# Separate semaphores for the output transposes of the last but one group in a cross-network kernel

## The chip, the cores and the metric

One NeuronCore of a Trainium2 chip. The metric is the device time of one execution in microseconds (us); lower is better. Before the change, three runs gave a median of 479.59 us (479.14 to 480.7). All were classed as fast; a one-core program whose run is within 1.5% of its fastest is classed so.

## The reference

A deep-and-cross network: 16384 rows of 416 features (bf16), six layers, each a full product with a 416 x 416 matrix, followed by a product and a sum element by element.

```python
B, F, D, L = 16384, 26, 16, 6          # Din = 26 * 16 = 416
def reference(x0, ws, bs):
    x = x0
    for l in range(ws.shape[0]):
        proj = jnp.einsum('bd,de->be', x, ws[l]) + bs[l]
        x = x0 * proj + x
    return x
```

## The kernel before

The rows are cut in 8 groups of 2048. A group is held transposed: features on the partitions (three tiles `t` of 128 features and a rest of 32), rows along the free dimension. TensorE multiplies, ScalarE adds the bias on the way out of PSUM, VectorE multiplies by `x0` and adds `x`. The pairs (group, layer) are interleaved, so that TensorE always has one to work on.

At the end of a group its result must be turned back, rows on the partitions. For groups 0 to 6 the DMA engines do this, with one transposing DMA for each feature tile into the staging tile `ost`, and one for the rest into `ot3`. Then `ost` is stored to HBM. Group 6 is "the last but one"; its store is cut in two column parts. Group 7, the last, is computed row-wise in its last layer, needs no turning, and is stored in five pieces.

```python
def output(g):
    s, s3 = xset[(g, L)], xtail[(g, L)]
    def turn(t):
        add("sp", lambda h: h.dma_start_transpose(
            ost[:, :, t * P:(t + 1) * P], xs[s][:, t * GC:(t + 1) * GC]),
            reads=[("x", s, t, j) for j in range(NJ)], writes=[("ost", t)], lane="ot", batch=g)

    turn(0)
    add("sp", lambda h: h.dma_start_transpose(ot3[:, :, :], x3s[s3][:, :]),
        reads=[("x3", s3)], writes=["ot3"], lane="ot3", batch=g)
    if g < LAST - 1:
        spread("pool")                        # ot3 -> the last 32 columns of ost
    turn(1)
    turn(2)
    if g < LAST - 1:
        store(g, 0, D, range(NT + 1))
    else:
        store(g, 0, 2 * P, (0, 1))            # first column part: 0..255, 1024 KB
    ...
# after the last tile of group 7, layer 4:
    spread("act")
    store(LAST - 1, 2 * P, D, (NT - 1, NT))   # second column part: 256..415, 640 KB
    ...                                       # last layer of group 7, row-wise:
    nat_store(0, 0, NJ)                       # three stores of 416 KB from SP, as they get done
    ...
        if j == 2:
            nat_store(kk, 0, 3)               # 312 KB from SP
    nat_store(kk, 3, 4, "act")                # 104 KB from ScalarE
```

A DMA's completion is counted on a semaphore per *lane*. The kernel assumes nothing about the order in which DMAs of the same lane and batch finish, so a count cannot tell them apart, and whoever needs one of them waits for the full count of the batch:

```python
for k, (key, ops) in enumerate(batches):
    n += 16 * len(ops)
    for op in ops:
        total[id(op)] = (n, ops)              # a wait for any op waits for all of its batch
```

SP (SyncE, which here only issues DMAs) works through its instructions in the order of the program: in the trace below it issues nothing from 461.19 to 464.71 us, while the first store of group 6 waits.

## Time and profile before

| quantity | before |
|---|---|
| median of 3 runs | 479.59 us |
| span of the profiled execution | 478.5 us |
| TensorE busy | 97% of the span |
| end of VectorE's last addition | 472.91 us |
| from there to the end of the span, called **the tail** below | 5.55 us |

The profile's page of the kernel before, the busy times by engine and the chain of waits that ended last:

```profile
PE 462.7 (97%) x3317; PEld 196.0 (41%) x3371; DVE 403.7 (84%) x696; ACT 342.3 (72%) x372; POOL 7.1 (1%) x15
...
PE 93%; DVE 2%; ACT 2%; issue 1%; POOL 0%; POOLq 0%
```

TensorE bounds the kernel as a whole. But the change is in the last microseconds, and there another limit holds. The timeline of the end, kernel before (start in us, length in us, engine, line, operation; SPq and ACTq are issues of DMAs, whose length is the time that the issuing engine spends on it, not the transfer):

```profile
456.79 4.40 SPq L637 DMA_TRANSPOSE ost<-x  x2
464.71 1.92 SPq L670 DMA_DIRECT2D out_dram<-ost  x2
466.67 6.85 SPq L866 DMA_DIRECT2D out_dram<-x  x4
...
472.53 0.38 DVE L859 TENSOR_TENSOR x<-x,x 128x416 bf16<-128x416 bf16 x1
472.94 0.37 ACTq L866 DMA_DIRECT2D out_dram<-x  x1
```

SP issues transposes 1 and 2 from 456.79 on (done with it at 461.19), then nothing until 464.71, then the two column parts of group 6 and four pieces of group 7. The waits of SP's DMA queue from 456 us on (who waited for what: us in total, times, longest):

```profile
SPq L670 <- DMA ost<-x: 3.5, 1, 3.5
```

The 3.5 us are the wait of the first column part for a transpose. By the completion records of the trace, transpose 1 landed at 461.22 us and transpose 2 at 464.70. The first part needs transposes 0 and 1 only.

The busy time by stretches of the end, kernel before (of use here are the last two columns: the mean busy share of the 16 DMA engines and GB/s; a packet that stands still counts as busy and packets overlap, so the share can pass 1, and the engines are taken as full here only where it is 1 or more and the GB/s are high too):

```profile
core 0: us, PE busy (x) PEld busy (x) DVE busy (x) ACT busy (x) POOL busy (x), PEclk, DMA share, GB/s
462.00:463.00 1.00, 1.00 (x17) 0.43 (x14) 0.78 (x2) 1.00 (x3) 0.00 (x0) 1.00 0.21 5
463.00:464.00 1.00, 1.00 (x13) 0.51 (x6) 0.97 (x3) 1.00 (x3) 0.00 (x0) 1.00 0.85 189
464.00:465.00 1.00, 1.00 (x7) 0.58 (x6) 0.90 (x2) 1.00 (x3) 0.00 (x0) 1.00 0.24 51
465.00:466.00 1.00, 1.00 (x13) 0.24 (x11) 0.83 (x3) 1.00 (x3) 0.00 (x0) 1.00 0.31 93
466.00:469.00 3.00, 3.00 (x23) 1.40 (x22) 2.93 (x6) 2.15 (x5) 0.00 (x0) 1.00 1.06 306
469.00:472.00 3.00, 1.76 (x11) 0.78 (x8) 2.57 (x6) 2.07 (x4) 0.00 (x0) 1.00 1.25 251
472.00:477.00 5.00, 0.00 (x0) 0.00 (x0) 0.87 (x3) 0.00 (x0) 0.00 (x0) 0.80 1.10 326
477.00:478.50 1.50, 0.00 (x0) 0.00 (x0) 0.00 (x0) 0.00 (x0) 0.00 (x0) 0.50 0.04 12
```

From 466 to 477 us the DMA engines are full without a break, and the last 4 us of that have no arithmetic at all. The end of the span is the end of that flow. Ahead of it are two poorer stretches: 462-463 (5 GB/s, a hole in the middle of transpose 2) and 464-466 (51 and 93 GB/s, between the end of transpose 2 and the first packets of the first store).

### The profile page before, as it was taken

The page shows a single profiled execution, that of the slowest core. Times are in us where ns is not written, and L with a number is a line of the kernel's source. Part 1 is how long each engine was busy: PE and PEld are TensorE (multiplying, and loading weights), DVE is VectorE, ACT ScalarE, POOL GpSimd, SP SyncE. Part 2 cuts the span into 40 slices and gives each one's busy share as a digit, 9 for nine tenths or more (in the row PEclk, how much of TensorE's full clock was granted, in tenths as well). Part 3 has the DMA queues.
Part 4 walks back from the last instruction along what each step waited for, and adds up shares of the span by engine and source line. Part 5 has one row for each costly group of instructions (what it writes and reads, how often), then busy time and mean ns, then how long its engine had stood idle before and what let it go on. Part 6 is the DMA issues. An engine that isn't in the chain of part 4 may idle for free.

```text
span 478.5 us, 8341 instructions
## 1 busy us (share of the span) xinstructions
PE 462.7 (97%) x3317; PEld 196.0 (41%) x3371; DVE 403.7 (84%) x696; ACT 342.3 (72%) x372; POOL 7.1 (1%) x15
## 2 busy tenths in 40 slices
PE   8999999999999999999999999999999999999993
PEld 6344444444443444444444444444444444434441
DVE  2888888888888888898889869888888888888894
ACT  4677777777777777777777777777777777767783
POOL 1000000000000000000000000000000000000000
PEclk9999999999999999999999999999999999999998
DMA  8986930730102477389219922870000237027889
GB/s 234 173 174 143 186 78 1 138 84 1 34 1 46 77 211 153 77 181 232 53 40 216 202 71 39 193 232 0 2 25 11 41 63 216 0 45 190 180 149 264
DMA packets 140379, 53.31 MB, mean 111 GB/s; under 512 B 114346, under 2 KB 139444, under 8 KB 140340
## 3 DMA queue, kind: packets, MB, share of 16 engines
q1 hardware_dynamic: 139592, 52.24, 49.0%
q10 hardware_dynamic: 748, 0.54, 0.4%
q8 instruction: 26, 0.43, 0.3%
q14 instruction: 13, 0.11, 0.1%
HBM read 5.97 MB, written 13.63 MB: 41 GB/s over the span
## 4 chain that ended last, share of the span: by engine, by line
PE 93%; DVE 2%; ACT 2%; issue 1%; POOL 0%; POOLq 0%
PE ps L456 75%; PE ps L477 7%; PE ps L497 6%; ACT tw L394 2%; PE ps L793 1%; PE ps L471 1%; DVE x L408 1%; PE ps L561 1%; DVE tw L403 1%; PE ps L541 1%; PE ps L488 1%; DVE x L859 0%; DVE x L853 0%; ACT x L565 0%; PE ps L804 0%
## 5 line engine op out<-in xcount | busy, mean ns | idle before, releaser
L394 ACT ACTIVATE tw<-ps,bias 128x1024 bf16<-128x1024 f32 (+1 forms) x295 | 299.8, 1071 | 119.8 <-PE ps L477 75.7
L456 PE MATMUL ps<-x,wm 128*128 128x512 bf16 x1638 | 372.2, 380 | 5.6 <-issue 3.7
L456 PEld LDWEIGHTS ps<-x,wm 128*128 128x128 bf16 x1692 | 159.1, 98 | 213.6 <-issue 28.8
L403 DVE TENSOR_TENSOR tw<-tw,x 128x1024 bf16<-128x1024 bf16 (+1 forms) x285 | 193.0, 686 | 53.4 <-ACT tw L394 53.1
L408 DVE TENSOR_TENSOR x<-tw,x 128x1024 bf16<-128x1024 bf16 (+1 forms) x285 | 181.9, 679 | 0.0
L477 PE MATMUL ps<-x,w 32*128 32x512 bf16 x512 | 39.2, 379 | 0.0
L497 PE MATMUL ps<-x,wm 128*32 128x512 bf16 x564 | 33.0, 380 | 0.0
L434 ACT ACTIVATE ts<-ps,bias 128x512 bf16<-128x512 f32 x47 | 28.8, 701 | 0.0
L438 DVE TENSOR_TENSOR x<-ts,x 128x512 bf16<-128x512 bf16 x47 | 18.8, 422 | 3.6 <-DMA x<-x 3.6
L497 PEld LDWEIGHTS ps<-x,wm 128*32 128x32 bf16 x564 | 13.8, 96 | 17.6 <-issue 5.3
L477 PEld LDWEIGHTS ps<-x,w 32*128 32x128 bf16 x512 | 7.8, 92 | 27.6 <-issue 27.1
L436 DVE TENSOR_TENSOR ts<-ts,x 128x512 bf16<-128x512 bf16 x47 | 18.7, 421 | 0.0
L663 POOL COPY ost<-ot 128x512 bf16<-128x512 bf16 x6 | 5.7, 943 | 422.6 <-DMA ot<-x 422.6
L793 PE MATMUL ps<-wm,x 128*128 128x416 bf16 x48 | 9.4, 340 | 0.0
L847 ACT ACTIVATE x<-ps 128x416 bf16<-128x416 f32 x16 | 7.7, 531 | 2.0 <-PE ps L793 1.9
L568 DVE COPY x<-ps 128x512 bf16<-128x512 bf16 x4 | 1.7, 425 | 8.8 <-PE ps L561 8.8
L565 ACT ACTIVATE x<-ps 128x512 bf16<-128x512 bf16 x8 | 4.2, 598 | 5.7 <-PE ps L561 5.7
L793 PEld LDWEIGHTS ps<-wm,x 128*128 128x128 bf16 x48 | 4.4, 98 | 4.1 <-issue 1.0
L488 PE MATMUL ps<-x,w 32*32 32x512 bf16 x188 | 5.9, 374 | 0.0
L471 PE MATMUL ps<-x,w 32*32 32x512 bf16 x208 | 5.6, 385 | 0.0
L561 PE MATMUL ps<-ident,x 128*128 128x128 bf16 x64 | 5.3, 243 | 0.3 <-ACT x L565 0.3
L853 DVE TENSOR_TENSOR x<-x,x 128x832 bf16<-128x832 bf16 (+1 forms) x9 | 4.9, 540 | 0.7 <-ACT x L847 0.6
(38 smaller groups left out, 35.9 us busy)
## 6 DMA issues: line engine op xcount, KB each, us to landing
out_dram<-ost SPq DMA_DIRECT2D x6, 1664.0 KB, 7.0
x<-in_x_dram SPq DMA_DIRECT2D x7, 416.0 KB, 8.0
x<-x SPq DMA_DIRECT2D x24, 96.0 KB, 2.2
wm<-in_ws_dram SPq DMA_DIRECT2D x5, 312.0 KB, 3.3
x<-x SPq DMA_DIRECT2D x22, 64.0 KB, 2.0
out_dram<-x SPq DMA_DIRECT2D x3, 416.0 KB, 5.6
out_dram<-ost SPq DMA_DIRECT2D x1, 1024.0 KB, 5.2
x<-ost SPq DMA_DIRECT2D x28, 32.0 KB, 2.3
```

Source lines behind the costliest of these rows:

```text
L394: add("act", lambda h, a=a, w=w, b0=b0: h.activation(tw[r][:, a * CH:(a + w) * CH], psum[:, b0 * CH:(b0 + w) * CH], ACT_F.Identity, bias=b ...
L403: add("dve", lambda h, a=a, e=e: h.tensor_tensor(tw[r][:, a * CH:e * CH], tw[r][:, a * CH:e * CH], x0s[s0][:, i * GC + a * CH:i * GC + e * ...
L408: add("dve", lambda h, a=a, e=e: h.tensor_tensor(xs[so][:, i * GC + a * CH:i * GC + e * CH], tw[r][:, a * CH:e * CH], src(i, a, e), ALU.ad ...
L434: add("act", lambda h: h.activation(ts[r][:, :], bank(b), ACT_F.Identity, bias=bias[:, 3, l:l + 1], scale=1.0), reads=[("ps", b), "bias"], ...
L436: add("dve", lambda h: h.tensor_tensor(ts[r][:, :], ts[r][:, :], x03, ALU.mult), reads=[("ts", r)] + tok0, writes=[("ts", r)], release=True)
L438: add("dve", lambda h: h.tensor_tensor(x3s[so][:, :], ts[r][:, :], res, ALU.add), reads=[("ts", r)] + rtok, writes=[("x3", so), ("x3", so, ...
L456: add("pe", lambda h, t=t, j=j: h.matmul(bank(banks[j]), wm[l][:, t, ecols], src(t, j, j + 1), start=(first and t == 0), stop=(not first a ...
L471: add("pe", lambda h, q=q, j=j, r=r, c=c, o=o: h.matmul(psum[o, banks[j] * CH:(banks[j] + 1) * CH], w3[l][q, i * P + c * T32:i * P + (c + ...
L477: add("pe", lambda h, q=q, j=j, r=r: h.matmul(bank(banks[j]), w3[l][q, ecols], src[q, :], start=first, stop=not first, tile_position=(r * ...
L488: add("pe", lambda h, l=l, b=b, s3=s3, ri=ri, qi=qi, ro=ro, qo=qo: h.matmul(psum[qo, b * CH:(b + 1) * CH], w3[l][qi, NT * P:D], s3[qi, :], ...
L497: add("pe", lambda h, t=t, j=j, src=src, l=l, b=b, ro=ro, qo=qo: h.matmul(psum[qo, b * CH:(b + 1) * CH], wm[l][:, t, NT * P:D], src(t, j, ...
L793: add("pe", lambda h, t=t: h.matmul(bank(b, n=D), xcol(t, j, kk), wm[l][:, t, :], start=(first and t == 0), stop=(not first and t == NT - 1)),
```

## The change

Intent: give each output transpose of group 6 its own semaphore, so that the first column part can wait for transposes 0 and 1 only, and go out earlier.

```diff
         def turn(t):
             add("sp", lambda h: h.dma_start_transpose(
                 ost[:, :, t * P:(t + 1) * P], xs[s][:, t * GC:(t + 1) * GC]),
-                reads=[("x", s, t, j) for j in range(NJ)], writes=[("ost", t)], lane="ot", batch=g)
+                reads=[("x", s, t, j) for j in range(NJ)], writes=[("ost", t)],
+                lane="ot" if g < LAST - 1 else f"ot_{t}", batch=g)
```

The order of instructions is the same on every engine; only waits differ. Below the change, line numbers are one higher (L670 becomes L671).

## The prediction

> **What bounds the kernel now.** Most of the span is TensorE: the page gives PE 97% busy, and the chain of waits is 93% PE. The change touches nothing there. It acts on the last 17 us. In the timeline the last matmul ends about 470.7 us and the last VectorE addition at 472.9, but the span ends at 478.5; the rest is output DMA. The windows view shows a DMA share of 1.06, 1.25 and 1.10 in 466-469, 469-472 and 472-477 us, at 306, 251 and 326 GB/s: from 466 to 477 all 16 DMA engines are full. So the tail is bound by the volume of the last seven stores (1024, 640, three of 416, 312 and 104 KB, 3.4 MB) and by when it starts to flow.
>
> **What starts it late.** The last but one group's three output transposes share one semaphore, and a wait is for its full count. In the trace's DMA records the second transpose (columns 128-255) lands at 461.2 us, the third at 464.7. The first store (columns 0-255, 1024 KB) needs only the first two, but is issued at 464.71, when the third lands; its first packets move at about 465.55. SP waits 3.5 us there (waits of the DMA queue).
>
> **What the change does.** No instruction is added, removed or moved; only waits differ. The first store waits for transposes 0 and 1; the second (columns 256-415) newly waits for transpose 2 beside ScalarE's spread copy, done at 460.1. SP pays for one or two more waits, at most 0.1 us. The first store can be issued when SP has issued the third transpose (461.19) and the second has landed: about 461.3, 3.4 us earlier. The second goes at about 464.75 instead of 465.15.
>
> **How much of 3.4 us survives.** The first store's packets stand behind the third transpose's in the same queue. The Trainium skill, "DMA: Bandwidth & Descriptors", section "Queues, rings and completion order", says that descriptors of one ring are taken in order; this trace agrees as far as it shows (a weight load issued behind a transpose began to move at 19.3 us, when the transpose's packets ran out). The third transpose's packets run until 464.4 us, with a hole at 461.9-463.1 (5 GB/s in the window 462-463) beside an instruction fetch. I expect the store not to fill it: in a like hole near 13 us ScalarE's queued copies stood still too. So the full stretch starts at 464.4 or slightly earlier instead of 465.55, and the same 3.4 MB follow at the same rates. Estimated gain: 1.15 us; up to 1 us more if the store does fill the hole. Above about 1.9 us nothing is left to win: the last stores are issued at 472.3 and 472.9, when their data is ready, and latency and their own transfer follow.
>
> **Prediction.** 478.4 us (gain 1.2 of 479.6, 0.25%), 8 in 10 between 477.4 and 479.5. Faster by over 2%: 0.01; within 2%: 0.985; slower by over 2%: 0.005.
>
> **What would show it.** First store issued near 461.3; second near 464.75, or up to 1 us later if the third transpose is delayed; DMA engines full from about 464.4; last landing about 476.7 instead of 477.9; PE, ACT and DVE unchanged up to 472.9.
>
> **What would make it wrong.** The third transpose slowed so much by the store's packets that the second store, and SP's queue behind it, is late and opens a hole; the store filling the hole (gain near 2 us); an instruction fetch at another moment; noise (479.1 to 480.7) larger than the gain.

## The result, and the profile after

| | before | after |
|---|---|---|
| median of 6 runs | 479.81 us | 478.80 us |
| lowest to highest | 479.14 to 480.70 | 478.15 to 479.41 |
| ratio of fast runs (95% interval) | | 0.998 (0.9966 to 0.9994) |
| span of the profiled execution | 478.5 | 477.6 |
| end of VectorE's last addition | 472.91 | 473.59 |
| tail | 5.55 us | 4.02 us |

A ratio is the mean time of one kernel's fast runs over the mean of the other's of the same rounds, so it is not quite the ratio of the medians. The change gains about 1 us, 0.2%.

The span falls by 0.85 us only, though the tail falls by 1.53. The rest, 0.68 us, is the start of this execution: TensorE waited 1.40 us for the first weights and began its first products at 7.66 us, against 6.60 us with no wait ahead of them in before. That is the lottery of the start (the runs of the experiments show how large it is), so from here on times are also given **relative to the end of VectorE's last addition**, which takes the start out.

The page after, the same two lines:

```profile
PE 462.0 (97%) x3317; PEld 195.7 (41%) x3371; DVE 404.1 (85%) x696; ACT 342.3 (72%) x372; POOL 6.5 (1%) x15
...
PE 92%; ACT 2%; DVE 2%; DMA 1%; issue 1%; ACTq 0%
```

The timeline of the end, after:

```profile
457.47 4.45 SPq L637 DMA_TRANSPOSE ost<-x  x2
462.02 0.97 SPq L671 DMA_DIRECT2D out_dram<-ost  x1
465.35 0.52 SPq L671 DMA_DIRECT2D out_dram<-ost  x1
465.92 7.37 SPq L867 DMA_DIRECT2D out_dram<-x  x4
...
473.21 0.38 DVE L860 TENSOR_TENSOR x<-x,x 128x416 bf16<-128x416 bf16 x1
473.62 0.37 ACTq L867 DMA_DIRECT2D out_dram<-x  x1
```

The first column part is now issued at 462.02 (less 0.68 for the start: 461.34 on the clock of before, against 464.71). The second part goes at 465.35, or 464.67 against 465.15. The waits of SP's DMA queue, after, the line that answers to the 3.5 us:

```profile
SPq L167 <- DMA ost<-x: 2.3, 1, 2.3
```

SP waits as before for transpose 2, but now only ahead of the second part (L167 is the helper's line for a separate wait instruction). The stretches of the end, after:

```profile
core 0: us, PE busy (x) PEld busy (x) DVE busy (x) ACT busy (x) POOL busy (x), PEclk, DMA share, GB/s
462.00:463.00 1.00, 1.00 (x16) 0.83 (x14) 1.00 (x3) 0.53 (x2) 0.00 (x0) 1.00 2.60 132
463.00:464.00 1.00, 1.00 (x14) 0.24 (x11) 0.78 (x2) 1.00 (x3) 0.00 (x0) 1.00 0.12 19
464.00:465.00 1.00, 1.00 (x7) 0.58 (x6) 0.97 (x3) 1.00 (x3) 0.00 (x0) 1.00 1.25 301
465.00:466.00 1.00, 1.00 (x7) 0.39 (x4) 0.76 (x3) 1.00 (x4) 0.00 (x0) 1.00 1.15 347
466.00:469.00 3.00, 3.00 (x29) 1.33 (x28) 2.90 (x6) 2.52 (x6) 0.00 (x0) 1.00 1.22 279
469.00:472.00 3.00, 2.45 (x20) 1.09 (x12) 2.60 (x5) 2.39 (x5) 0.00 (x0) 1.00 1.22 265
472.00:476.00 4.00, 0.00 (x0) 0.00 (x0) 1.52 (x5) 0.00 (x0) 0.00 (x0) 1.00 1.12 332
476.00:477.60 1.60, 0.00 (x0) 0.00 (x0) 0.00 (x0) 0.00 (x0) 0.00 (x0) 0.58 0.05 14
```

The poor stretch between the transpose and the stores is gone: 301 and 347 GB/s from 464 to 466. The hole in transpose 2 is still there (463-464, 19 GB/s) and is not filled, although the first store had been issued at 462.02. (The share of 2.60 in 462-463, at only 132 GB/s, is no full flow: packets of the transpose stood still there for up to 1.5 us each by their records.)

The trace records every DMA packet with its start, queue and size. Worked out from these records, for this kernel and all that follow (us relative to the end of VectorE's last addition; "98%" is when 98% of the store packets have started; "fetch" is the start of the 16 KB instruction fetches in the last 24 us):

```
run            tail  transpose 2  transposes'  first store  98% of  last    fetch
                     landed       last packet  packet       them    packet
before         5.55  -8.21        -8.70        -7.25        3.82    4.39    -11.40
after          4.02  -8.31        -8.79        -8.83        2.17    2.91    -11.36
e0_after       3.95  -8.38        -8.87        -8.91        2.10    2.84    -11.47
e10_after      4.21  -8.08        -8.58        -8.62        2.39    3.11    -11.15
e1_wait_all    5.46  -8.34        -8.83        -7.33        3.74    4.30    -11.41
e2_one_store   4.40  -8.15        -8.63        -7.13        2.77    3.22    -11.45
e3_no_first    2.52  -8.21        -8.70        -7.20        1.29    1.56    -11.36
e4_act_queue   3.96  -8.35        -8.84        -8.88        2.12    2.86    -11.43
e5_rows        3.62  -8.90,-8.08  -8.61        -7.89        2.01    2.53    -11.63
e6_fetch       3.79  -9.26        -9.75        -9.93        1.29    2.67    -20.07, -3.76
e7_rows_fetch  3.59  -10.37,-9.18 -9.64        -9.37        1.34    2.49    -20.02, -2.55
e8_fewer       4.49  -7.25        -9.27        -9.87        1.66    3.39    -9.26
e9_rows_fewer  3.26  -10.41,-7.80 -8.38        -8.43        1.55    2.17    -10.56
```

(Where the third transpose was cut in two halves, both landings are given.) The first two lines hold the explanation. Before, the stores' first packet came 1.45 us after the transposes' last one: 0.49 us until the completion was seen (-8.70 to -8.21), the rest from there through the issue to the first packet (-7.25). After, it comes as the transpose runs out, with no gap (16 of the store's packets start before the transpose's last one). The flow of the 3.41 MB of stores takes the same time in both: 11.64 us before (-7.25 to 4.39) and 11.74 us after (-8.83 to 2.91). So the tail is shorter by the shift of the flow's start, 1.58 us, less the 0.10, and with 0.05 us less from the last packet to the end of the span: 1.53.

Each tail is read from one profiled execution. How well it repeats can be seen from the kernels with the same flow: 5.55 and 5.46 in before and e1_wait_all, 3.95 to 4.21 in the three traces of the changed kernel and in e4_act_queue.

### The profile page after: what moved, and what is told of

Its sections match the earlier page's. It is cut to its first block, busy times and chain, and to the rows that moved or that the text cites. A ratio compares the mean times of both kernels' runs of the same rounds, so it can differ in the third digit from the quotient of the medians.

```text
span 477.6 us, 8343 instructions
## 1 busy us (share of the span) xinstructions
PE 462.0 (97%) x3317; PEld 195.7 (41%) x3371; DVE 404.1 (85%) x696; ACT 342.3 (72%) x372; POOL 6.5 (1%) x15
## 4 chain that ended last, share of the span: by engine, by line
PE 92%; ACT 2%; DVE 2%; DMA 1%; issue 1%; ACTq 0%
PE ps L456 75%; PE ps L477 7%; PE ps L497 6%; ACT tw L394 2%; DMA wm<-in_ws_dram 1%; PE ps L794 1%; PE ps L471 1%; DVE x L408 1%; DVE tw L403 1%; PE ps L488 1%; PE ps L561 0%; DVE x L860 0%; DVE x L854 0%; ACT x L565 0%; PE ps L805 0%
```

## The experiments

Two explanations stood against each other. **Theory A**: the end is the end of a DMA flow of fixed volume at the rate of its packets; the change gains the idle time before the flow. **Rivals**: B, the semaphores matter by themselves; C, SP's in-order queue sets the end, and the change gains because SP gets to the last group's stores earlier. Later came the hole in the third transpose: D, the instruction fetch that lies in it causes it; E, it is the transpose's own. Eleven runs were made, in three calls on chips 5, 7 and 5; each call shares its runs of the kernel before (medians 480.35, 480.44 and 480.14 us). All their executions were fast (e4_act_queue has four, e9_rows_fewer five, the others six).

### e0_after and e10_after: the changed kernel again

No edit.

> The changed kernel again, for an interval beside the other runs of this chip. Theory A (the tail is bound by the volume of the stores; the change gains the 1.15 us in which the DMA engines stood empty before the first store, and a little rate): about 1.2 to 1.5 us below before, ratio 0.997. The tail, from the end of VectorE's last addition to the end of the span, was 5.5 us before and 4.0 after; it should be 4.0 again, whatever the start of the run does.

> The changed kernel once more, as the neighbour of these two on the same chip: tail 4.0, ratio 0.997.

Measured: medians 479.01 and 479.68 us, ratios 0.997 (0.9945 to 0.9995) and 0.998 (0.9951 to 1.0008), tails 3.95 and 4.21. The gain repeats in the tail. In time the medians lie 1.34 and 0.46 us below those of before, and the second interval holds 1.0. What also shows is how noisy the start is. VectorE's last addition ended at 472.33 us in the first and at 474.95 us in the second, 2.6 us apart in the same kernel. TensorE's first products in the timeline of e0_after (start, length):

```profile
6.38 1.46 PE L456 MATMUL ps<-x,wm 128*128 128x512 bf16 x6
```

The same six products in the timeline of e10_after, with the idle time ahead of them and what ended it:

```profile
7.56 2.72 PE L456 MATMUL ps<-x,wm 128*128 128x512 bf16 x6 [0.79 <-DMA wm<-in_ws_dram]
```

In the second they start 1.2 us later, after a wait for the first weights, and the same six matmuls then take nearly twice as long. The runs of e10_after spread from 477.54 to 481.8 us. A difference of 1 us in the tail is clear in one trace, and hardly so in six times.

### e1_wait_all: the semaphores without the earlier issue

```diff
-            store(g, 0, 2 * P, (0, 1))
+            store(g, 0, 2 * P, (0, 1, 2))
```

> The change's three semaphores, but the first store waits for all three. Theory A (the earlier issue of the first store is the whole gain): as before, ratio 1.000, tail 5.5 us, first store issued when the third transpose lands, packets about 0.85 us later. Rival B (the separate semaphores or the other wait counts matter by themselves, for example by ending a wait sooner on SP or by a moved start of the run): as the change, ratio 0.997, tail 4.0.

Measured: 479.86 us, ratio 0.9983 (0.9964 to 1.0001), tail 5.46, first store packet at -7.33. The tail and the packets are those of before, with three semaphores in place. So B falls, by the trace: the earlier issue is the change's gain in the tail. The times would not settle it: the ratio of 0.9983 is about the change's own 0.998, its interval holds 1.0, and the median lies 0.49 us below that of before although the tail is that of before, which shows what the noise can do.

### e2_one_store: the same start, larger packets

In the kernel before, the two column parts are made one store:

```diff
-            store(g, 0, 2 * P, (0, 1))
+            pass
...
-    store(LAST - 1, 2 * P, D, (NT - 1, NT))
+    store(LAST - 1, 0, D, range(NT + 1))
```

> The kernel before, with the two stores of the last but one group made one of 1664 KB (packets of 832 bytes in place of 512 and 320), issued when the third transpose has landed. Theory A (volume at the rate of its packet size): in before the 1024 KB took about 3.4 us and the 640 KB 2.7 us of full DMA engines; 1664 KB at the 331 GB/s of the 832 byte packets take 5.15 us, so 0.9 us less: ratio 0.998, tail about 4.6 us, with the start of the flow as late as before. Rival C (what counts is when SP can issue the last group's stores, and the change gained because SP's queue is freed earlier): SP issues the last group's stores about 0.4 us earlier than in before, so at most 0.4 us.

Measured: 479.35 us, ratio 0.9974 (0.995 to 0.9997), tail 4.40, so 1.15 us shorter than before, where 0.9 was expected. The flow starts as late as in before (-7.13), but it takes 10.35 us in place of 11.64. The stretches of e2_one_store show why:

```profile
466.00:469.00 3.00, 3.00 (x26) 1.35 (x23) 2.90 (x6) 2.46 (x5) 0.00 (x0) 1.00 1.01 334
469.00:472.00 3.00, 2.07 (x12) 0.95 (x10) 2.60 (x6) 2.07 (x4) 0.00 (x0) 1.00 1.08 339
```

These are 334 and 339 GB/s with full engines, where before had 306 (512 byte packets) and 251 (mostly 320 byte packets). So the column cut, whose purpose is an earlier start, costs more than 1 us in packet size, and in the kernel before it bought nothing for it. Against C the run is not clean: SP issued the last group's first store at -7.65 here against -6.23 in before, 1.4 us earlier and not 0.4. What rules C out comes with e5_rows.

### e3_no_first: the floor

The changed kernel without the first store; its result is wrong (256 columns of group 6 stay unwritten).

```diff
-            store(g, 0, 2 * P, (0, 1))
+            pass
```

> Wrong result on purpose: the first store (1024 KB) is left out of the changed kernel, to find the floor. Theory A: the tail no longer has a full DMA queue and ends by the last issues (their data ready at the end of VectorE's last addition): tail about 3 us, so about 2.5 us below before, ratio 0.995, and only 1 us below the changed kernel. If the tail falls far more, the last stores' latency was overestimated; if it does not fall below 4.0, the change already took all there is.

Measured: 477.17 us, ratio 0.9926 (0.9908 to 0.9945), tail 2.52, rather less than the 3 expected. The stretches of e3_no_first show that the engines ran dry before the last pieces came:

```profile
472.00:473.00 1.00, 0.00 (x0) 0.00 (x0) 0.83 (x3) 0.00 (x0) 0.00 (x0) 1.00 0.13 39
473.00:474.50 1.50, 0.00 (x0) 0.00 (x0) 0.00 (x0) 0.00 (x0) 0.00 (x0) 1.00 0.83 284
```

With a third of the volume gone, the flow no longer sets the end; the data of the last stores does. So 2.5 us is about the floor that any rearrangement of group 6's stores can reach, and the changed kernel, at 4.0, is 1.5 us above it.

### e4_act_queue: the first store on another queue

The first store is issued by ScalarE, on its own queue, in a moment where ScalarE idles:

```diff
-            store(g, 0, 2 * P, (0, 1))
+            pass
...
     turn_tails([b0, b1, b2, b3])
+    store(LAST - 1, 0, 2 * P, (0, 1), "act")      # store() given an engine argument
```

> The changed kernel, but the first store is issued by ScalarE, on its own DMA queue, just after its copy of the turned tails (its idle moment at about 11.5 us before the end of VectorE's last addition), with the same two waits. Theory A1 (the first store is held back by its place in SP's queue behind the third transpose): on another queue its packets interleave with the transpose's, fill the 1.2 us hole, and the flow is full about 1 us earlier: tail about 3.0 us. Rival A2 (the hole stops all queues, as it stopped ScalarE's copies near 13 us): packets start only when the transpose's start again, about 9.8 us before the end of the last addition; the third transpose lands later; tail about 3.6 to 4.0 us. In both ScalarE loses 0.4 to 1 us in its last stage, which may move the last addition itself by as much.

Measured: 478.53 us (4 runs), ratio 0.996 (0.9936 to 0.9984), tail 3.96, and ScalarE lost nothing that moved the last addition. The issue, in the timeline of e4_act_queue:

```profile
461.14 0.41 ACTq L671 DMA_DIRECT2D out_dram<-ost  x1
```

That is -11.61 relative to the last addition. Its first packet moved at -8.88, 2.7 us later, just as the last packet of transpose 2 had started (-8.84). So A1 falls and A2 is nearer, but even A2 expected packets from -9.8 on, mixed with the second half of the transpose; until -8.88 there were none. So the place in SP's queue is not what held this store back.

It would be too much to say that a store always waits for a transpose in flight. The traces show other cases. At the start of the kernel before, 32 packets of a weight load that ScalarE issued run from 15.47 to 15.74 us with 234 packets of a transpose that SP issued (from HBM) started between them. The DMA queues of before in 15.4 to 15.8 us, SP's (q1) and ScalarE's (q10): packets, MB, share:

```profile
q1 hardware_dynamic: 367, 0.09, 103.2%
q10 hardware_dynamic: 48, 0.03, 21.8%
```

And in e8_fewer, below, 193 packets of the first store start before the last packet of transpose 2. What makes the difference is not shown.

The Trainium skill, "DMA: Bandwidth & Descriptors", section "Issuing engines are not separate DMA queues", says that DMAs of all issuing engines interleave on the same 16 engines. For these two, one a transpose, the trace shows hardly any (the table's -8.84 and -8.88: 16 of the store's 2048 packets start before the transpose's last); for the weight load above it shows it.

### e5_rows: cut by rows, not by columns

The third transpose in two halves of 1024 rows, each with its own semaphore, then two stores of full rows:

```diff
-        turn(2)
-        ... store(g, 0, 2 * P, (0, 1))
+            for r in range(2):
+                add("sp", lambda h, r=r: h.dma_start_transpose(
+                    ost[:, r * 8:(r + 1) * 8, 2 * P:3 * P],
+                    xs[s][:, 2 * GC + r * GC // 2:2 * GC + (r + 1) * GC // 2]),
+                    reads=[("x", s, 2, j) for j in (2 * r, 2 * r + 1)],
+                    writes=[("ost2", r)], lane=f"ot_2{r}", batch=g)
...
-    store(LAST - 1, 2 * P, D, (NT - 1, NT))
+    store_rows(LAST - 1, 0)       # rows 0..1023 of the group, all 416 columns, 832 KB
+    store_rows(LAST - 1, 1)
```

> The changed kernel with the last but one group cut by rows in place of columns: the third transpose in two halves of 1024 tokens each with its own semaphore, then two stores of 832 KB with full rows (packets of 832 bytes), the first after the first half. Theory A (volume at the rate of its packet size, from the moment it can start): the flow starts as in the changed kernel, at the end of the third transpose's packets or slightly later, and 3.4 MB at 331 GB/s take 10.3 us in place of 11.2: tail about 3.1 us, 0.9 below the changed kernel, not far from the floor of 2.5; ratio about 0.995. Rival C (SP's queue): the second half's store is issued as late as the changed kernel's second store, so tail 4.0.

Measured: 478.30 us, ratio 0.995 (0.9932 to 0.9967), tail 3.62 (expected 3.1). The flow took 10.42 us as expected for 832 byte packets, but it began at -7.89 and not at about -8.8. The first half of the transpose lies across the hole and landed at -8.90 only, so the first store was issued at -8.82, too late to follow the transposes without a gap.

This run rules out C. SP issued the first two of the last group's stores at -7.64 and -5.23 here, and at -7.65 and -5.24 in e2_one_store; the later ones are issued when their data is ready, in both. Yet the tail is 3.62 against 4.40, a difference of 0.78, and the flow starts 0.76 earlier (-7.89 against -7.13). What counts is when the flow starts and how long it takes.

e5_rows has the lowest ratio to before of the kernels with a right result, and beats before clearly of noise; its interval overlaps those of the changed kernel and of e4_act_queue. It was not run on the same chip as the changed kernel; by the tails it is 0.3 to 0.6 us better (3.62 against 3.95 to 4.21).

### e6_fetch: the instruction fetch moved

57 tiny matmuls with no reader are put at the start of TensorE's program, in place of 12 of its warming matmuls:

```diff
-    keep_busy(14, 7)
+    for _ in range(57):
+        add("pe", lambda h: h.matmul(bank(7, n=2)[0:2, :], ones[:, 0:2], ones[:, 0:2], start=True, stop=True),
+            reads=["ones"], writes=[("ps", 7)])
+    keep_busy(2, 7)
```

> The changed kernel with 57 tiny matmuls (2 by 2 results that nobody reads) put first on TensorE in place of 12 of its warming matmuls, so that its instruction fetches (one of 16 KB for each 256 of its instructions, by the count of both) come some 90 instructions earlier. The last fetch, in both kernels at about 11.4 us before the end of VectorE's last addition, in the middle of the third transpose, should fall near 14 to 15 us before it, where the DMA engines have nothing to do. Theory D (the 1.2 us hole in the third transpose is caused by that fetch): no hole, the third transpose lands about 1.2 us earlier (at -9.5), the first store flows from about -10.0, tail about 2.8 us. Rival E (the hole belongs to the transpose itself, and the fetch only happens to lie there): hole and tail as in the changed kernel, 4.0. The start of the run may be up to 1 us longer by the tiny matmuls, so the tail is what decides.

The idea came from the packet records: a packet of 16 KB of the queue named "instruction" starts at 461.5 us in the kernel before, and the hole of the transpose follows it. There are 26 such packets in an execution, one for each 256 of TensorE's instructions (by the records' count of matmuls and weight loads between two of them, in the mean). The Trainium skill, "Runtime: NRT & Kernel Launch", section "Instruction fetch mechanics", says the same: instructions are fetched in blocks of 16 KiB, 256 of them, over DMA.

Measured: 479.83 us, ratio 0.9993 (0.997 to 1.0016), tail 3.79. D was right about the hole: with the fetch moved to -20.07, the third transpose runs through and lands at -9.26 in place of -8.31. The stretches of e6_fetch:

```profile
462.00:463.00 1.00, 0.70 (x10) 0.57 (x11) 1.00 (x4) 0.24 (x1) 0.00 (x0) 1.00 1.14 222
463.00:464.00 1.00, 1.00 (x12) 0.63 (x10) 0.87 (x2) 0.87 (x3) 0.00 (x0) 1.00 1.15 211
...
475.00:476.00 1.00, 0.00 (x0) 0.00 (x0) 0.00 (x0) 0.00 (x0) 0.00 (x0) 0.50 0.81 267
476.00:477.00 1.00, 0.00 (x0) 0.00 (x0) 0.00 (x0) 0.00 (x0) 0.00 (x0) 0.50 0.08 23
```

The middle of the transpose now runs at 222 and 211 GB/s, without a hole. The flow starts at -9.93, and 98% of it has started by 1.29 against 2.17 in the changed kernel. But the tail falls by 0.2 us, not by 1.2. The added instructions had brought on a 27th fetch, at -3.76, in the middle of the stores, and the last 2% of the packets trail by 1.38 us (1.29 to 2.67; in the changed kernel 0.74). The expected gain came and was given back at the end. (23 GB/s, the rate of the trailing packets, is about a sixteenth of the full flow's 332.) The start of this execution was longer as well (last addition at 474.25 us), so the times show nothing.

### e7_rows_fetch: both

The edits of e5_rows and e6_fetch together.

> Rows in place of columns, and the moved fetch, together. Theory A with D: both savings would sum to 2.1 us, but the floor found by leaving out a store is a tail of 2.5 us, as the last stores are issued when VectorE's last additions end; so tail 2.5 to 2.7, about 1.4 below the changed kernel, ratio to before about 0.994, if the start of the run is not longer. If D falls, the same as the rows alone.

Measured: 479.37 us, ratio 0.9976 (0.9957 to 0.9994), tail 3.59, no better than the rows alone (3.62). The third transpose's halves landed at -10.37 and -9.18, and the flow started at -9.37 and had 98% of its packets started at 1.34. But again a fetch fell into the stores (-2.55), and the last packet started at 2.49 only. So the expected 2.5 to 2.7 was missed.

### e8_fewer and e9_rows_fewer: the fetch moved the other way

20 warming matmuls are left out, on the changed kernel and on e5_rows; that takes 40 instructions away.

```diff
-    keep_busy(14, 7)
+    keep_busy(2, 7)
...
-        keep_busy(8, 3)
```

> The changed kernel with 20 of its warming matmuls left out (12 of the first 14, and the 8 before the first product), so 40 TensorE instructions fewer and every later fetch 40 instructions later. Theory D (the hole in the third transpose is the instruction fetch): the last fetch moves from about 11.4 us to about 10 us before the end of VectorE's last addition, to the end of the third transpose or behind it, and no new fetch comes before the end, as one did at -3.75 us when instructions were added. So the third transpose lands at about -9.3 as with the added instructions, the first store flows from about -10. If a fetch only delays the one DMA engine that carries it, that engine still has its sixteenth of the stores to move 1 us later, so the tail falls to between 2.8 and 3.6 us; if the late fetch was the reason for the missing microsecond, nearer 2.8. Rival E (the hole is the transpose's own): 4.0. The cold start may cost some tenths before 10 us.

> Rows in place of columns, and the 20 warming matmuls left out: the candidate that should beat both kernels. The flow starts at about -9.5 us, 3.4 MB at 331 GB/s need 10.3 us, so the engines run out of work about when the last stores are issued; the fetch at about -10 leaves one engine 1 us behind, with time to make it up in the queue's gaps. Tail 2.5 to 2.9 us, so 2.6 to 3.0 below before if the start is not longer: ratio 0.994. If the tail stays at 3.6 as with rows and added instructions, the late fetch was not what held that one back.

Measured, e8_fewer: 481.22 us, ratio 1.0013 (0.9997 to 1.0028), tail 4.49, longer than the changed kernel's, against an expectation of 2.8 to 3.6. The fetch fell at -9.26, on the last packets of the third transpose. There was no hole for all, but the transpose's completion came at -7.25, 2 us after its last packet had started (0.5 us in the others), and the stores' last 2% trailed by 1.73 us. The end of e8_fewer, in stretches:

```profile
476.00:477.00 1.00, 0.00 (x0) 0.00 (x0) 0.00 (x0) 0.00 (x0) 0.00 (x0) 0.52 0.88 258
477.00:478.00 1.00, 0.00 (x0) 0.00 (x0) 0.00 (x0) 0.00 (x0) 0.00 (x0) 0.50 0.07 22
478.00:479.30 1.30, 0.00 (x0) 0.00 (x0) 0.00 (x0) 0.00 (x0) 0.00 (x0) 0.50 0.02 5
```

For 2.3 us next to nothing moves (1.5 us in before, from 477 us on), and the end waits for it.

Measured, e9_rows_fewer: 480.70 us, ratio 1.0011 (0.9995 to 1.0027), tail 3.26, the shortest of all with a right result, but above the 2.5 to 2.9 expected. Its fetch (-10.56) fell into the second half of the transpose and made the hole there. It is not the better kernel: VectorE's last addition ended at 475.63 us (474.90 in e8_fewer). Nearly all runs of both lie above the median of before (480.14), so the shorter tail of e9_rows_fewer is lost at the start. That the missing warming matmuls are the cause is likely but not shown, for e10_after, which has them, also had a start as long once (474.95).

In sum, D stands as far as the hole goes: the third transpose had it in every kernel whose fetch fell into its body, and did not have it in the three where the fetch fell elsewhere or on its last packets. The same shows earlier in before: fetches at 12.6 and 265.9 us fall into transposes that load the input, and some 0.3 to 0.5 us later the transposes all but stop for 1.4 and 1.2 us (5 and 6 GB/s). (It is not always a full stop: at two fetches of e6_fetch, at 54.9 and 221.5 us, the transposes go on at about a quarter of their rate for 2 us.) But a fetch among the stores was no cheaper: in the three kernels that had one (e6_fetch, e7_rows_fetch, e8_fewer) the last 2% of the packets trailed by 1.15 to 1.73 us, against 0.74 or less in the others, and the gain was lost. That the trailing packets are those of the one DMA engine that carried the fetch is a guess, for the records name no engine. It fits their rate: 21 to 23 GB/s in the last stretches of the three kernels, where one of 16 engines' share of the full 332 would be about 21.

## Why the prediction was right

- **Size.** Predicted 478.4 us, in a range of 477.4 to 479.5; measured 478.80. The gain was predicted as 1.2 us and was 1.0 by the medians, 1.53 in the tail. "Within 2%" held. That the median came so near is in part luck: the gain by the medians was 1.0, 1.34 and 0.46 us in the three measurements of the changed kernel.
- **The bound.** That the tail is a full DMA flow of fixed volume was right. The flow took 11.64 us before and 11.74 after, so a shift of its start came through to the end nearly whole. e2_one_store (same start, faster flow, shorter tail), e5_rows (same issues by SP as e2_one_store, earlier flow, tail shorter by as much) and e3_no_first (less volume) all answer to it.
- **How much of 3.4 us survives.** The first store was issued 3.4 us earlier, as predicted (461.34 on the clock of before, against "about 461.3"), and gained 1.5, because its packets start only when the transpose's run out. That the hole would not be filled was right too.
- **A term that was mis-sized.** The idle time ahead of the flow was put at 1.15 us ("464.4 or slightly earlier instead of 465.55"), read in steps of half a microsecond. The packet records give 1.45 us: the last transpose packet at -8.70 and the first store packet at -7.25, that is 464.21 and 465.66. (The weight load that the prediction saw begin at 19.3 us began at 19.46 by the same records.)
- **A ceiling that was too low.** The prediction held that above about 1.9 us nothing is left to win. The floor run has a tail 3.03 us shorter than before, and e9_rows_fewer, with a right result, one 2.29 us shorter.
- **A reason that did not hold.** The prediction put the wait for the transpose's end down to the place in "the same queue", with the skill's ring order for it. e4_act_queue had the store on another queue and gave the same first packet, at the same distance. The effect was right; ring order is not needed for it.
- **The rest.** The second store at 464.67 (predicted 464.75), the last landing at 476.44 (predicted 476.7), both on the clock of before. TensorE, ScalarE and VectorE worked as before, but 0.68 us later, by the start of the run, which the prediction had counted only as noise.

What stays open: why the issued store waits until the transpose runs out, on another queue too, while the weight load did not; why a fetch stops a transpose; and how much of the 1.5 us between the changed kernel and the floor can be had in a kernel whose fetch falls where no DMA is wanted.

## What to carry to other kernels

When a kernel ends in a full DMA flow, look for the packet before it and ask what the first store waits for. An earlier issue is worth only the idle time of the DMA engines that it removes (here 1.45 of 3.4 us), and a cut that makes it possible must be weighed against the packet size that it costs: one uncut store gained 1.15 us in the tail, nearly as much as the change, and a cut by rows, which keeps full rows, gained more than either (1.93 us, in one trace). With differences of 0.3%, measure from a mark late in the program, such as the last addition, so that the lottery of the start drops out.

## What the Trainium skill lacked or had wrong

- "Runtime: NRT & Kernel Launch", section "Instruction fetch mechanics", calls the cost of crossing a 16 KiB block mostly hidden. For the fetching engine it may be. Here a fetch stopped a DMA transpose for about 1.2 us (5 GB/s in 462-463 in before; gone when the fetch was moved), and one among the stores left the last 2% of packets trailing by 1.15 to 1.73 us, against 0.74 or less without.
- "DMA: Bandwidth & Descriptors", section "Issuing engines are not separate DMA queues": the interleaving that it states did not happen, but for 16 packets, between a transpose issued by SP and a store issued by ScalarE 2.7 us ahead of its own first packet (-11.61 to -8.88, with the transpose's last packet at -8.84). It did happen for a weight load at the start (15.47 to 15.74 us in before). No page that was found says when a plain DMA is held back by a transpose in flight.
- "DMA: Bandwidth & Descriptors", section "Why small descriptors are slow (HBM only)", works out the overhead for descriptors of 256 bytes alone, and no page that was found has measured rates of trn2 stores by packet size. Stores from SBUF to HBM moved, with full engines, at about 250 GB/s with packets of mostly 320 bytes, 306 with 512, and 334 to 339 with 832.
